# Decoding w_out's chunks into PSUM, transposing their finished high and low parts, and queueing the router's products further behind

## The chip, the cores and the metric

The kernel runs on one core of one Trainium2 chip. The metric is the device time of one execution in microseconds (us); a time of a kernel is the median of its runs. The engines are named as in the profile: PE (TensorE's matmuls), PEld (its weight loads), DVE (VectorE), ACT (ScalarE), POOL (GpSimd), SP (SyncE, which only issues transfers here).

## The reference, cut to what matters

Three layers follow one another: attention with a sliding window of 128 and 4 sink positions over 4 x 8 heads, 768 positions and 64 features; an MLP with a normalization; and a routed MLP with 8 experts, one per token.

```
x = attention(q, k, v)                      # (3072, 512)
h = x @ w_in                                # (3072, 1024)
solu = h * softmax(h)
ln = (solu - mean) / sqrt(var + 1e-6) * g_ln
x2 = ln @ w_out                             # (3072, 512)
logits = x2 @ w_gate                        # (3072, 8)
e = argmax(logits); gate = softmax(logits)[e]
out = gate * (relu(x2 @ w1[e]) @ w2[e])
```

`w_in` and `w_out` arrive as 64-bit floating-point numbers, seen as pairs of 32-bit integers, and the kernel has to turn them into 32-bit numbers itself.

## The kernel before, in words

Products that need nearly full 32-bit accuracy are made of three matmuls in the type fp32r on a high and a low part of each operand (high x high, high x low, low x high); the low part is the number less its rounded high part. Attention works on 32 units (128 query rows times three for two heads); a unit n has six score matmul groups `s` (lines 225, or 228 and 229 from unit 5 on), each followed on DVE by `copy_predicated` (L232) and a masked maximum (L233) and on ACT by an exponential (L235). The first MLP works on 24 tiles of 128 tokens (`m_in`: L453 to L455, `m_act`, `m_tr`: L502, `m_out`: L523 to L525), and the routed MLP comes last.

The weights of the first MLP are decoded while attention starts: `load_w_in` in eight chunks, then `load_w_out` in eight chunks of 128 x 512. `decode` loads a chunk (L333, issued from ACT's queue), scales its low words on ACT (L350) and joins them with the high words in two DVE instructions (L351 into the PSUM tile `dt`, L352 into the result). For `w_in` the result is a PSUM tile `dh`, for `w_out` an SBUF tile `dec`. ACT then rounds the high part (L362 for `wih`; L397, with `g_ln` as a factor by row, for `woh`), and DVE makes the low part (L363 `wil`, L398 `wol`).

Eight more columns of `woh` and `wol` carry `w_out @ w_gate`, so that the router's logits come out of the same matmuls as `x2`. They are made in two steps. `logits` transposes a decoded chunk (four fp32 transposes, L376) and copies it out on ACT (`xt`, L378). `logits2` multiplies it with `w_gate` (four fp32 matmuls of 8 columns, two records each in the trace, L384) and writes the eight columns (L387, L388 on DVE). In the loop over chunks, chunk k's step runs `logits2` of chunk k-2 and `logits` of chunk k-1; the last pieces come when the first `m_out` asks for them.

One table sets when the decoding's steps are written: `W_AT` lists after which exponential of attention each step comes (`weigh`), and its position fixes the L350 of a step behind that exponential. Within that program order a scheduler with a timeline of its own orders the instructions of each engine; on the chip each engine works through its list in that order. PSUM has 8 banks: 3 with the tag `psa` for attention's tiles (`s`, `skp`, `tp`, `av`), 5 with `psm` for the rest (`h`, `lt`, `x2`, `wt`, `wt2`, `dt`, `dh`). `skp` is the tile of the sink transposes (L270); ACT (L271) and DVE (L272, `skt`) read it before its bank is free.

Of the kernel before, what the change touches and what calls it, by code (L numbers as in the profile page):

```python
# [8 lines left out]
F32 = mybir.dt.float32  # L9
F32R = mybir.dt.float32r  # L10
BF16 = mybir.dt.bfloat16
I32 = mybir.dt.int32
U32 = mybir.dt.uint32
AF = mybir.ActivationFunctionType
ALU = mybir.AluOpType
# [15 lines left out]
WB, DB, EB, NXR, XGB = 4, 4, 2, 2, 6  # L31
PA = 3
NATP, LEAD = 5, 4
KLV = 2
LA = 2
TE = 18
# [1 line left out]
XT = 21  # L38
WSB = 6
HG, HD, HSTEP, FH = 1, 5, 2, 1  # L40
W_AT, RATIO = [1, 4, 7, 10, 13, 16, 19, 22, 24, 26, 27, 29, 30, 32, 33, 35], 0.7
ROOM = [608, 576, 512, 416, 384, 320, 288, 128]
CAPS = [-(-n // 128) * 128 for n in ROOM]
NBLK = sum(CAPS) // 128
# [4 lines left out]
SC_IN, SC_OUT, SX = 2.0 ** 8, 2.0 ** 64, 2.0 ** -8  # L49
# [3 lines left out]
def raw(ap):  # L53
    return ap.bitcast(F32)
# [3 lines left out]
def body(ctx, tc, a):  # L58
    nc = tc.nc
    V, A, G, T, SY = nc.vector, nc.scalar, nc.gpsimd, nc.tensor, nc.sync  # L60
# [3 lines left out]
    const = ctx.enter_context(tc.tile_pool(name="const", bufs=1))  # L64
# [18 lines left out]
    def ps(name):  # L83
        if name in ATT:
            a_ = True
        elif name in MOE:
            a_ = False
        else:
            flip[0] += 1
            a_ = flip[0] % 8 < PA  # L90
        return ps_p.tile([128, 512], F32, tag="psa" if a_ else "psm", name=name, bufs=PA if a_ else 8 - PA)
# [4 lines left out]
    ident = const.tile([128, 128], F32, name="ident")  # L96
# [45 lines left out]
    def in_win(out, r, tmp):  # L142
# [7 lines left out]
                           op1=ALU.mult)  # L150
# [30 lines left out]
    def a_split(n):  # L181
# [9 lines left out]
        A.activation(out=qA, in_=qd, func=AF.Copy)  # L191
        (V if n < KLV else G).tensor_tensor(out=kl, in0=kd, in1=raw(kA), op=ALU.subtract)
        G.tensor_tensor(out=lA, in0=qd, in1=raw(qA), op=ALU.subtract)  # L193
# [122 lines left out]

    g_sb = const.tile([128, 8], F32, name="g_sb")
    g_s = const.tile([128, 8], F32, name="g_s")
    g_l = const.tile([128, 8], F32, name="g_l")
    wg_sb = const.tile([128, 4, NE], F32, name="wg_sb")  # L320

    dec_p = [at]

    def dec_tile(name):
        return dec_p[0].tile([128, 512], I32, tag="dec", name=name, bufs=DB)

    ex, pin = [], [None]

    def decode(src, sb, flush):

        w = dec_p[0].tile([128, 512, 2], I32, tag="w64", name="w64", bufs=WB)
        with tc.issue_after(first_d.ins) if dec_p[0] is at else ExitStack():
            A.dma_start(out=w, in_=src)  # L333
        lo, hi = w[:, :, 0], w[:, :, 1]
        t0 = ps("dt").bitcast(I32)
        y = ps("dh") if sb is None else sb
        if flush:
            t = dec_tile("dec")
            V.tensor_scalar(out=t0, in0=hi, scalar1=0x07FFFFFF, scalar2=3, op0=ALU.bitwise_and,
                            op1=ALU.logical_shift_left)  # L340
            V.scalar_tensor_tensor(out=t, in0=hi, scalar=-0x40000000, in1=t0, op0=ALU.bitwise_and,
                                   op1=ALU.bitwise_or)
            A.activation(out=lo, in_=lo.bitcast(U32), func=AF.Copy, scale=2.0 ** -29)
            G.tensor_tensor(out=t, in0=t, in1=lo, op=ALU.add)
            x = ps("dh")
            A.activation(out=x, in_=hi.bitcast(F32), func=AF.Abs)
            V.scalar_tensor_tensor(out=y, in0=x, scalar=E_MIN, in1=t.bitcast(F32), op0=ALU.is_ge, op1=ALU.mult)
        else:
            with tc.issue_after(pin[0].ins) if pin[0] else ExitStack():
                A.activation(out=lo, in_=lo.bitcast(U32), func=AF.Copy, scale=LOW3)  # L350
            V.scalar_tensor_tensor(out=t0, in0=hi, scalar=3, in1=lo, op0=ALU.logical_shift_left, op1=ALU.bitwise_xor)  # L351
            V.scalar_tensor_tensor(out=y.bitcast(I32), in0=hi, scalar=-0x80000000, in1=t0, op0=ALU.bitwise_and,  # L352
                                   op1=ALU.bitwise_xor)
        return y
# [11 lines left out]

    def load_w_out(flush=False):
        sc = SC_OUT * (1.0 if flush else RAW)
        V.tensor_scalar(out=g_s, in0=g_sb, scalar1=sc, scalar2=None, op0=ALU.mult)
        V.tensor_scalar(out=g_l, in0=g_sb, scalar1=1.0 / SC_OUT, scalar2=None, op0=ALU.mult)  # L370

        def logits(k, x):

            t = ps("wt")
            for d in range(4):
                T.transpose(t[:, 128 * d:128 * d + 128], x[:, 128 * d:128 * d + 128], ident)  # L376
            xt = dec_tile("xt").bitcast(F32).rearrange("p (a b) -> p a b", a=4)
            A.activation(out=xt, in_=t.rearrange("p (a b) -> p a b", a=4), func=AF.Copy, scale=sc)  # L378
            return k, xt

        def logits2(k, xt):
            t = ps("wt2")
            for d in range(4):
                T.matmul(t[:, 0:NE], xt[:, d, :], wg_sb[:, d, :], start=(d == 0), stop=(d == 3))  # L384
            wp = t[:, 0:NE]
            gk = g_l[:, k:k + 1]
            V.tensor_scalar(out=woh[:, k, 0, 256:264], in0=wp, scalar1=gk, scalar2=None, op0=ALU.mult)  # L387
            V.scalar_tensor_tensor(out=wol[:, k, 0, 256:264], in0=wp, scalar=gk, in1=raw(woh)[:, k, 0, 256:264],  # L388
                                   op0=ALU.mult, op1=ALU.subtract)

        last = last2 = None
        for k in range(8):
            x = dec_tile("dec").bitcast(F32)
            decode(a["w_out"].bitcast(I32)[128 * k:128 * k + 128, :], x, flush)
            h_ = woh[:, k, :, 0:256]
            p2 = x.rearrange("p (a b) -> p a b", a=2)
            A.activation(out=h_, in_=p2, func=AF.Copy, scale=g_s[:, k:k + 1])  # L397
            V.scalar_tensor_tensor(out=wol[:, k, :, 0:256], in0=p2, scalar=g_s[:, k:k + 1], in1=raw(h_),  # L398
                                   op0=ALU.mult, op1=ALU.subtract)
            if last2:  # L400
                logits2(*last2)
                last2 = None
            if last:
                last2 = logits(*last)
            last = (k, x)
            yield 1.5
        logits2(*last2)
        logits2(*logits(*last))


    tri = const.tile([128, 128], BF16, name="tri")
# [871 lines left out]
    def weights():  # L1283
        yield from load_w_in()
        yield from load_w_out()
# [35 lines left out]
    wn = [0]  # L1321

    def weigh():
        while wn[0] < 16 and len(ex) > W_AT[wn[0]]:
            pin[0] = ex[W_AT[wn[0]]]
            step(gw, "w")
            wn[0] += 1
# [4 lines left out]
    while done_x[0] < 0:  # L1332
        step(ga, "a")
        cnt_ += 1
        if cnt_ == 12:
            late_loads()
        weigh()
# [4 lines left out]
    while True:  # L1342
        if a_open and ta <= tm * RATIO:
            d = step(ga, "a")
# [7 lines left out]
        d = step(gm, "m")  # L1352
# [7 lines left out]
        else:  # L1360
            d = step(ga, "a")
# [61 lines left out]
```

## Time and profile before

| | us |
|---|---|
| median of 3 runs (817.53 to 819.14) | 819.07 |
| the profiled execution's own time | 819.58 |
| its span in the trace | 817.4 |
| outside of the span | 2.2 |

How to read the profile: an engine's busy time is the time in which its instructions ran; a row's idle time is what the engine stood still just before it, with the instruction that released it. PEclk is the granted clock of TensorE as a share of 2.4 GHz; 0.50 is the lower level, 1.2 GHz. Matmuls are pipelined, so the cost of one in a row of equal ones is the distance from start to start, not the duration printed for it. "issue" as a releaser means that the profile shows nothing that the engine waited for.

### The profile page before, as it was taken

To read this page: it belongs to the slowest core of one execution; us is meant where nothing else is said; L and a number is where in the kernel's file an instruction comes from. 1 tells how busy PE (TensorE), PEld (TensorE's weight loads), DVE (VectorE), ACT (ScalarE), POOL (GpSimd) and SP (SyncE) were. 2 spreads that over 40 slices of the span, in tenths; PEclk is the share of its full clock that TensorE was granted. 3 is DMA by queue.
4 is the path that set the end of the run, shared out by engine and by line. 5 is a ranking of instruction groups with operands and counts; after the bars stand their busy time and mean duration, and the time that the engine had idled before them with its cause. 6 is when DMAs were issued, how large, how long until landed. Compare 5 with 4: busy or idle time off the path is not lost.

```text
span 817.4 us, 15512 instructions
## 1 busy us (share of the span) xinstructions
PE 776.4 (95%) x5003; PEld 670.3 (82%) x5003; DVE 478.5 (59%) x1766; ACT 461.9 (57%) x1236; POOL 355.4 (43%) x393
## 2 busy tenths in 40 slices
PE   4779999999999998999999998999999999999996
PEld 2457788897988887888988898888978888989885
DVE  6898666676758647766776566426333443435541
ACT  3677686675757848657766374235425243436442
POOL 3565354545354544555433121156235244535533
PEclk9968999999999999999999999999999999999998
DMA  8585355567557457474530271195375416663650
GB/s 272 186 260 155 92 150 119 131 135 142 126 132 156 117 113 161 121 154 102 142 85 27 32 239 44 46 330 204 101 254 193 156 63 213 225 211 96 227 172 28
DMA packets 78281, 120.82 MB, mean 148 GB/s; under 512 B 14122, under 2 KB 52524, under 8 KB 78192
## 3 DMA queue, kind: packets, MB, share of 16 engines
q1 hardware_dynamic: 70512, 97.48, 44.5%
q0 software_dynamic: 5088, 13.88, 4.8%
q10 hardware_dynamic: 2592, 8.39, 3.0%
q8 instruction: 42, 0.69, 0.4%
q14 instruction: 47, 0.39, 0.2%
HBM read 80.61 MB, written 13.28 MB: 115 GB/s over the span
## 4 chain that ended last, share of the span: by engine, by line
PE 78%; DVE 9%; DMA 5%; issue 3%; ACT 2%; POOL 1%; POOLq 0%; SPq 0%; ACTq 0%; DVEq 0%
PE ht L853 6%; PE ht L854 6%; PE ht L852 6%; PE x L523 5%; PE y L922 5%; PE h L453 5%; PE y L924 5%; PE y L923 5%; PE x L525 5%; PE x L524 5%; PE h L454 5%; PE av L306 4%; PE h L455 4%; PE s L228 3%; PE s L229 2%
## 5 line engine op out<-in xcount | busy, mean ns | idle before, releaser
L523 PE MATMUL x<-woh,lh 128*128 128x264 f32 (+1 forms) x384 | 111.5, 290 | 0.1
L525 PE MATMUL x<-woh,ll 128*128 128x264 f32 (+1 forms) x384 | 109.5, 286 | 0.0
L524 PE MATMUL x<-wol,lh 128*128 128x264 f32 (+1 forms) x384 | 109.0, 284 | 0.0
L235 ACT ACTIVATE P<-P,mx 128x144 f32<-128x144 f32 x192 | 78.5, 411 | 49.3 <-DVE mx L233 46.9
L760 ACT ACTIVATE wh<-wst 128x1024 fp32r<-128x1024 f32 x64 | 67.5, 1058 | 45.9 <-PE ht L853 26.6
L768 POOL TENSOR_TENSOR wl<-wst,wh 128x1024 fp32r<-128x1024 f32 x28 | 67.8, 2423 | 55.1 <-ACT wh L760 48.1
L853 PE MATMUL ht<-xel,wh 128*128 128x288 f32 (+5 forms) x256 | 81.2, 318 | 0.0
L854 PE MATMUL ht<-xeh,wl 128*128 128x288 f32 (+5 forms) x256 | 81.0, 318 | 0.0
L453 PE MATMUL h<-wih,bxh 128*128 128x512 f32 x192 | 79.0, 412 | 1.0 <-DVE ll L506 0.9
L768 DVE TENSOR_TENSOR wl<-wst,wh 128x1024 fp32r<-128x1024 f32 x36 | 53.1, 1478 | 45.9 <-ACT wh L760 44.0
L852 PE MATMUL ht<-xeh,wh 128*128 128x288 f32 (+5 forms) x256 | 79.7, 318 | 0.0
L922 PE MATMUL y<-wh,hh 128*128 128x512 f32 x192 | 77.2, 402 | 1.2 <-DVE hl L861 1.2
L454 PE MATMUL h<-wil,bxh 128*128 128x512 f32 x192 | 76.4, 398 | 0.0
L924 PE MATMUL y<-wh,hl 128*128 128x512 f32 x192 | 75.5, 395 | 0.0
L923 PE MATMUL y<-wl,hh 128*128 128x512 f32 x192 | 75.2, 392 | 0.0
L455 PE MATMUL h<-wih,bxl 128*128 128x512 f32 x192 | 74.3, 399 | 0.0
L523 PEld LDWEIGHTS x<-woh,lh 128*128 128x128 f32 x384 | 72.4, 188 | 1.7 <-DVE r L556 0.3
L232 DVE COPY_PREDICATED s<-pick,s 128x128 f32<-128x128 int32 x160 | 45.2, 292 | 48.6 <-PE s L229 45.9
L524 PEld LDWEIGHTS x<-wol,lh 128*128 128x128 f32 x384 | 72.4, 189 | 0.7
L525 PEld LDWEIGHTS x<-woh,ll 128*128 128x128 f32 x384 | 72.3, 189 | 0.6 <-issue 0.3
L193 POOL TENSOR_TENSOR lA<-qd,qA 128x384 fp32r<-128x384 f32 x27 | 28.1, 1042 | 95.3 <-ACT qA L191 75.0
L244 POOL TENSOR_TENSOR pk<-P,sm 128x768 f32<-128x768 f32 x32 | 47.6, 1487 | 45.2 <-DVE sm L242 38.8
(275 smaller groups left out, 2046.5 us busy)
## 6 DMA issues: line engine op xcount, KB each, us to landing
wst<-w SPq DMA_DIRECT2D x64, 512.0 KB
x_d<-xrow SPq DMA_DIRECT2D x24, 264.0 KB
qd<-qT SPq DMA_DIRECT2D x32, 192.0 KB
qB<-qA SPq DMA_DIRECT2D x54, 96.0 KB
lB<-lA SPq DMA_DIRECT2D x54, 96.0 KB
kd<-kx SPq DMA_DIRECT2D x16, 280.0 KB
w<-w_in ACTq DMA_DIRECT2D x8, 512.0 KB
w<-w_out ACTq DMA_DIRECT2D x8, 512.0 KB
```

The source lines that it names most:

```text
L453: T.matmul(h, xh[k], wih[:, k, cs], start=(k == 0), stop=False)
L454: T.matmul(h, xh[k], wil[:, k, cs], start=False, stop=False)
L523: T.matmul(p[:, 0:n], lh[:, k, :], woh[:, k, c, 0:n], start=(k == 0), stop=False)
L524: T.matmul(p[:, 0:n], lh[:, k, :], wol[:, k, c, 0:n], start=False, stop=False)
L525: mm = T.matmul(p[:, 0:n], ll[:, k, :], woh[:, k, c, 0:n], start=False, stop=(k == 7))
L768: return (G if c % 2 and r else V).tensor_tensor(out=l_, in0=st_w.pop((r, which, c)), in1=raw(h_), op=ALU.subtract)
L852: T.matmul(o, wh[:, k, fs], xh(k), start=(k == 0), stop=False)
L853: T.matmul(o, wh[:, k, fs], xl(k), start=False, stop=False)
L854: T.matmul(o, wl[:, k, fs], xh(k), start=False, stop=(k == 3))
L922: T.matmul(o, hh[:, k, sl], wh, start=(k == 0), stop=False)
L923: T.matmul(o, hh[:, k, sl], wl, start=False, stop=False)
L924: T.matmul(o, hl[:, k, sl], wh, start=False, stop=(k == 7))
```

## The change

Four things change. `decode` now puts `w_out`'s chunks into PSUM (`dh`), as it did `w_in`'s, and L397 and L398 read them there (L399 and L400 in the changed kernel). The four fp32 transposes of a decoded chunk become eight fp32r matmuls against an identity `ident_r`, two for each 128 columns, that add the finished high and low parts while transposing them (L378 in the changed kernel). `g_ln` is then already in the product, so the factor `g_l` goes. And the loop runs 8 + LAG steps with LAG = 3: `logits2` of chunk k-3, then `logits` of chunk k-1; three steps that have no chunk are written behind the exponentials 37, 38 and 40.

```
+LAG = 3
-W_AT, RATIO = [1, 4, ..., 33, 35], 0.7
+W_AT, RATIO = [1, 4, ..., 33, 35, 37, 38, 40], 0.7
...
     def load_w_out(flush=False):
         sc = SC_OUT * (1.0 if flush else RAW)
+        ident_r = dec_p[0].tile([128, 128], F32R, tag="idr", name="ident_r")
+        V.tensor_copy(ident_r, ident)
         V.tensor_scalar(out=g_s, in0=g_sb, scalar1=sc, scalar2=None, op0=ALU.mult)
-        V.tensor_scalar(out=g_l, in0=g_sb, scalar1=1.0 / SC_OUT, scalar2=None, op0=ALU.mult)
-        def logits(k, x):
+        def logits(k):
             t = ps("wt")
             for d in range(4):
-                T.transpose(t[:, 128 * d:128 * d + 128], x[:, 128 * d:128 * d + 128], ident)
+                for n, w in enumerate((woh, wol)):
+                    T.matmul(t[:, 128 * d:128 * d + 128], w[:, k, d // 2, 128 * (d % 2):128 * (d % 2) + 128], ident_r,
+                             start=(n == 0), stop=(n == 1))
...
-            A.activation(out=xt, in_=t.rearrange("p (a b) -> p a b", a=4), func=AF.Copy, scale=sc)
+            A.activation(out=xt, in_=t.rearrange("p (a b) -> p a b", a=4), func=AF.Copy)
...
-        last = last2 = None
-        for k in range(8):
-            x = dec_tile("dec").bitcast(F32)
-            decode(a["w_out"].bitcast(I32)[128 * k:128 * k + 128, :], x, flush)
...
-            if last2:
-                logits2(*last2)
-                last2 = None
-            if last:
-                last2 = logits(*last)
-            last = (k, x)
+        done = []
+        for k in range(8 + LAG):
+            if k < 8:
+                x = decode(a["w_out"].bitcast(I32)[128 * k:128 * k + 128, :], None, flush)
...
+            if k >= LAG:
+                logits2(*done.pop(0))
+            if 0 < k < 9:
+                done.append(logits(k - 1))
             yield 1.5
-        logits2(*last2)
-        logits2(*logits(*last))
```

Two places show what this does to the lists of the engines. The first is PE's list where attention passes from unit 4 (the last `s` with `kd,qd`) to unit 5 (the first with `kA,qA`). Before:

```order
L376 MATMUL wt_577<-ident_78,dec_549 128x128 x4
L270 MATMUL skp_616<-ident_78,psk_415 128x128 x3
L225 MATMUL s_622<-kd_445,qd_444 128x272
L225 MATMUL s_627<-kd_445,qd_444 128x272
L384 MATMUL wt2_598<-wg_sb_127,xt_582 128x8 x4
L376 MATMUL wt_605<-ident_78,dec_568 128x128 x4
L228 MATMUL s_729<-kA_679,qA_675 128x272
```

The same place now (the pairs of `woh` and `wol` into wt_577 come four times):

```order
L271 MATMUL skp_617<-ident_78,psk_414 128x128 x3
L226 MATMUL s_623<-kd_444,qd_443 128x272
L226 MATMUL s_628<-kd_444,qd_443 128x272
L378 MATMUL wt_577<-ident_r_546,woh_70 128x128
L378 MATMUL wt_577<-ident_r_546,wol_71 128x128
...
L378 MATMUL wt_602<-ident_r_546,woh_70 128x128
L229 MATMUL s_734<-kA_684,qA_680 128x272
L229 MATMUL s_771<-kB_685,qB_681 128x272
L230 MATMUL s_771<-kB_685,lB_683 128x272
L378 MATMUL wt_602<-ident_r_546,wol_71 128x128
```

The first chunk's transposes moved behind `skp` and the last two `s` of unit 4, its products with `w_gate` moved out of this place, and the second chunk's transposes are split around the first `s` of unit 5.

The second place is DVE's list at the same time, from the low part of `w_out`'s first chunk to `skt`, which frees the bank of `skp`. Before:

```order
L398 SCALAR_TENSOR_TENSOR wol_71<-dec_549,g_s_125,woh_70 128x2x256
L312 SCALAR_TENSOR_TENSOR bxl_530<-wt_520,bxh_529 128x384
L232 COPY_PREDICATED s_622<-pick_121,s_622 128x128
L352 SCALAR_TENSOR_TENSOR dec_589<-w64_590,dt_592 128x512
L232 COPY_PREDICATED s_627<-pick_121,s_627 128x128
L398 SCALAR_TENSOR_TENSOR wol_71<-dec_568,g_s_125,woh_70 128x2x256
L387 TENSOR_SCALAR woh_70<-wt2_598,g_l_126 128x8
L272 TENSOR_TENSOR skt_615<-skp_616,skt_615 128x384
```

The same place now:

```order
L400 SCALAR_TENSOR_TENSOR wol_71<-dh_552,g_s_125,woh_70 128x2x256
L233 COPY_PREDICATED s_623<-pick_121,s_623 128x128
L313 SCALAR_TENSOR_TENSOR bxl_529<-wt_519,bxh_528 128x384
L351 SCALAR_TENSOR_TENSOR dt_595<-w64_593 128x512
L233 COPY_PREDICATED s_628<-pick_121,s_628 128x128
L273 TENSOR_TENSOR skt_616<-skp_617,skt_616 128x384
```

The third chunk's second decoding step, the second chunk's low part and the first logits' copy moved behind `skt`, and the third chunk's first decoding step (ahead of the first row of the list before) now stands between the two.

## Rows read from the trace of the kernel before

**Rows 1.** The page: span, and PE's busy time, share and instructions.
```profile
span 817.4 us, 15512 instructions
PE 776.4 (95%) x5003; PEld 670.3 (82%) x5003; DVE 478.5 (59%) x1766; ACT 461.9 (57%) x1236; POOL 355.4 (43%) x393
```

**Rows 2.** Busy time by stretch: length, engines (instructions), granted clock, DMA share, GB/s.
```profile
46.00:83.00 37.00, 30.72 (x180) 25.86 (x177) 32.62 (x90) 26.12 (x69) 23.58 (x23) 0.77 0.72 202
83.00:460.00 377.00, 370.21 (x2611) 320.70 (x2610) 248.98 (x1111) 254.25 (x788) 175.54 (x210) 1.00 0.52 120
```

**Rows 3.** Whom PE waited for, 46 to 83 us: us in total, times, longest.
```profile
PE s L228 <- issue: 3.4, 1, 3.4
PE wt L384 <- ACT xt L378: 1.3, 2, 0.7
PE skp L270 <- POOL psk L253: 1.0, 1, 1.0
PE s L228 <- DVE mx L233: 0.5, 1, 0.5
```

**Rows 4.** PE's timeline: start, us, operation, shape, count, [idle before it, releaser].
```profile
50.35 0.63 PE L376 MATMUL wt<-ident,dec 128*128 128x128 f32 x4
54.40 0.57 PE L228 MATMUL s<-kA,qA 128*128 128x272 f32 x1 [3.41 <-issue]
...
66.25 0.63 PE L376 MATMUL wt<-ident,dec 128*128 128x128 f32 x4
66.64 0.47 PE L453 MATMUL h<-wih,bxh 128*128 128x512 f32 x1
...
73.82 1.06 PE L384 MATMUL wt<-wg_sb,xt 128*128 128x8 f32 x8 [0.51 <-ACT xt L378]
...
76.12 1.87 PE L384 MATMUL wt<-wg_sb,xt 128*128 128x8 f32 x8 [0.75 <-ACT xt L378]
...
110.10 0.28 PE L523 MATMUL x<-woh,lh 128*128 128x264 f32 x1
...
111.19 0.29 PE L523 MATMUL x<-woh,lh 128*128 128x264 f32 x1
```

**Rows 5.** DVE's timeline around the stall of PE.
```profile
49.88 1.21 DVE L398 SCALAR_TENSOR_TENSOR wol<-dec,g_s,woh 128x512 fp32r<-128x512 f32 x1
...
51.67 0.68 DVE L352 SCALAR_TENSOR_TENSOR dec<-w,dt 128x512 int32<-128x512 int32 x1
...
52.47 1.23 DVE L398 SCALAR_TENSOR_TENSOR wol<-dec,g_s,woh 128x512 fp32r<-128x512 f32 x1
53.62 0.21 DVE L387 TENSOR_SCALAR woh<-wt,g_l 128x8 fp32r<-128x8 f32 x1
53.76 0.54 DVE L272 TENSOR_TENSOR skt<-skp,skt 128x384 fp32r<-128x384 f32 x1
```

**Rows 6.** PE alone by stretches of 1 us, where the granted clock changes (columns: PE, clock, DMA).
```profile
52.00:53.00 1.00, 0.00 (x0) 0.50 1.02 377
62.00:63.00 1.00, 1.00 (x11) 0.90 1.00 316
76.00:77.00 1.00, 0.88 (x5) 0.50 0.09 29
82.00:83.00 1.00, 1.00 (x4) 0.66 0.76 173
```

**Rows 7.** The high and low parts of both weights: ns min/median/max, first and last start.
```profile
L398 DVE SCALAR_TENSOR_TENSOR wol<-dec,g_s,woh x8: 739/790/1595, 49.9 to 81.1; 128x512 fp32r<-128x512 f32 x8
L363 DVE SCALAR_TENSOR_TENSOR wil<-dh,wih x8: 676/684/691, 13.8 to 47.7; 128x512 fp32r<-128x512 f32 x8
L397 ACT ACTIVATE woh<-dec,g_s x8: 707/722/731, 47.3 to 80.4; 128x512 fp32r<-128x512 f32 x8
L362 ACT ACTIVATE wih<-dh x8: 572/592/597, 13.2 to 45.5; 128x512 fp32r<-128x512 f32 x8
```

**Rows 8.** DVE groups of 46 to 83 us: count, busy us, mean ns, idle before.
```profile
L398 DVE SCALAR_TENSOR_TENSOR wol<-dec,g_s,woh 128x512 fp32r<-128x512 f32 x8 | 7.9, 982 | 0.9 <-ACT woh L397 0.9
```

## What was predicted, ahead of the run

> **What bounds the kernel now.** I began with the busy times. PE is busy for 776.4 of 817.4 us [rows 1], so the end is PE's list: its work plus the time in which it stands or runs at the lower clock. The view by stretches tells where that second part lies. From 83 to 460 us, where attention and the first MLP run side by side, PE is busy for 370.21 of 377 us at a granted clock of 1.00; from 46 to 83 us, where w_out is decoded, it is busy for 30.72 of 37 us at 0.77 [rows 2]. So whatever the change does early moves the end almost one for one, because PE has no slack behind it, and there are two things to look at in the 37 us: 6.3 us of idle time and the clock.
>
> The idle time has four owners [rows 3]. The largest is one gap of 3.4 us. The profile gives it no releaser, but PE's timeline and DVE's tell one. PE finishes the transposes of 50.35 at 50.98 and starts the first score of unit 5 at 54.40 [rows 4]; `skt` on DVE ends at 53.76 + 0.54 = 54.30 [rows 5]. `skp` and the last two scores of unit 4 hold the three banks of attention, so the next score needs the bank that `skt` frees, and `skt` stands on DVE behind two low parts of w_out and a decoding step. The second owner is 1.3 us in which the router's products wait for `xt`, twice, at 73.82 (0.51) and 76.12 (0.75) [rows 4]: transposes, ACT's copy, products, transposes, copy, products, one after the other with little else in the list.
>
> The clock falls to the lower level twice. After PE had been less than fully busy and then idle, it reads 0.50 from 52 us on and comes back in the stretch of 62 us (0.90); after the two waits for `xt` it reads 0.50 from 76 us and comes back within the stretch of 82 us (0.66) [rows 6]. A reading of 0.90 between 0.50 and 1.00 means a return at 62.2, one of 0.66 a return at 82.7.
>
> **The change part by part.** All sums are of the profiled execution (819.58 us, of which 817.4 are the span), which lies 0.5 us above the median.
>
> *New work on PE.* 32 transposes go, 64 fp32r products of 128 columns come. Four transposes take 66.64 - 66.25 = 0.39 us from start to start, 0.098 us each, at full clock [rows 4]. The trace has no fp32r product of 128 columns. The nearest row with the same weight load is the `x` product with 264 columns: nine in 111.19 - 110.10 = 1.09 us, 0.121 us each [rows 4]. This is the upper end; the lower end is the transpose's 0.098, which loads and streams a block of the same shape. I take 0.11, in the middle, since the columns are as few as the transpose's and the weight type is that of `x`. 64 x 0.11 - 32 x 0.098 = 7.0 - 3.1 = **+3.9 us** (3.1 to 4.6). The products with `w_gate` stay as many.
>
> *The gap of 3.4 us.* In the new list three things no longer stand ahead of `skt` [rows 5]: the third chunk's second decoding step, 0.68 us of which some 0.6 are not covered by the next instruction's start; the second chunk's low part from 52.47 to 53.62, 1.15; the logits' copy from 53.62 to 53.76, 0.14. The first low part, 1.21 us long here, shrinks by 0.5 (next paragraph). `skt` begins at about 53.76 - 1.9 - 0.5 = 51.4 and PE resumes at 52.0 instead of 54.4: **-2.4 us**. What is late next: the new transposes of the second chunk stand right behind that score, and need the second low part, which now follows `skt` on DVE and ends at about 52.9. Ends: 0, if the next DVE result is as late as `skt` was, and -3.4.
>
> *Low parts and high parts out of PSUM.* With the chunk in SBUF a low part took 0.739 to 1.595 us, 7.9 us for eight, mean 0.982 [rows 7, 8]; the same instruction on w_in's chunks, which lie in PSUM, took 0.676 to 0.691 in all eight cases [rows 7]. DVE gains 8 x (0.982 - 0.684) = 2.4 us, ACT 8 x (0.722 - 0.592) = 1.0 us [rows 7]. DVE is busy for 32.62 of these 37 us [rows 2], so the first is worth something, but only through PE's waits, and it is not counted again beside them. The copy that makes `ident_r` (a third of `skt`'s width, so under 0.54 us [rows 5]) comes once, ahead of the first transposes, where DVE's idle 4.4 us of the stretch can hide it; without that cover it would cost its own length.
>
> The Trainium skill's page "Perfetto Trace Analysis", section "Optimizing Scalar/DVE Operations", speaks against this part: it gives VectorE a larger fixed cost per instruction on PSUM (about 125 ns) than on SBUF (about 60 ns). By it the eight low parts would take 0.5 us more in all, an estimate from that page; rows 7 say the opposite for this very instruction, whose slowest run from PSUM is faster than the fastest from SBUF, and the measurement decides.
>
> *The queue for the router.* With the products three chunks behind, `xt` is made long before they come up: the waits of 0.51 and 0.75 go, **-1.3 us**. A new one can take their place: the transposes needed only the decoded chunk, and now need its high part (0.59 us on ACT) and its low part (0.68 us on DVE) as well [rows 7], 1.3 us later. Behind a waiting transpose on PE stand scores and `h` products, and DVE waits for those scores. Ends: 0, and 2.6 us for two such waits in full; I take one of half that size, **+0.7 us**, since the transposes still come one step behind their chunk.
>
> *The clock.* In the first slow stretch PE restarts 2.4 us sooner; if the return comes as much sooner, 2.4 us of work at half rate become 1.2: **-1.2 us**. Ends: 0, and -3.9 if the clock did not fall at all, half of the 62.2 - 54.4 = 7.8 us that PE then worked. The second stretch, 82.7 - 76 = 6.7 us, cost 3.35 us. It follows the waits for `xt`, which go, but other gaps may stand there; I take half, **-1.7 us**, ends 0 and -3.4.
>
> *The steps that moved.* The three added steps hold products and their copies only, no transfers; w_out's loads stay in ACT's queue in the old order. All the router's work is now ahead of the first `x` product, before which some of it was queued; the number of instructions ahead of the end is the same either way, so this is 0.
>
> Sum: 3.9 - 2.4 - 1.3 + 0.7 - 1.2 - 1.7 = **-2.0 us**. DVE allows it: 2.4 us less of work and 4.4 us of idle time in a stretch that has to shrink by 3.5 us, since about 1.5 us of the new PE work come behind it.
>
> **The rivals.** *The clock holds.* If the filled gaps keep PE at the upper level all along, both slow stretches vanish: -2.0 - (3.9 - 1.2) - (3.4 - 1.7) = -6.4, 812.7 us. For it: both falls came after gaps that the change fills. Against it: the first came a mere 1.0 us after PE ran dry at 50.98 [rows 4], and at that point the new list is hardly fuller than the old. The Trainium skill's page "TensorE: Matmul & The Clock Gate", section "Part 4: PE-mode transpose", has a rule that would lead here: transposes do not bring the engine to full clock, and the new ones are ordinary products. No row here shows the one without the other.
>
> *The gap moves.* DVE, busy at 88% here [rows 2], still hands out the banks late; the transposes' wait takes the place of the waits for `xt`, and the second slow stretch stays: 3.9 - 2.4 - 1.3 + 0.7 - 1.2 = -0.3, 818.8 us.
>
> *Slower: a bank too few.* The chunk now holds a `psm` bank from its second decoding step to the end of its low part. Five banks serve `dt`, `dh`, `wt`, `wt2` and the two `h` tiles that start at 66.64 [rows 4]. If a late low part keeps an `h` or a decoding step without a bank, PE waits for one high and low part, 1.3 us [rows 7], at each of the last three chunks, and these gaps keep the second slow stretch: -2.0 + 3.9 + 1.7 = +3.6, 822.7 us. It decides once idle time and lost clock from 46 us to the end of the decoding shrink by less than the 3.9 us of new work. Against it: w_in's chunks lived in the same banks without a long wait of PE, but then no `h` did.
>
> **How the numbers follow.** The forecast is 819.07 - 2.0 = 817.1 us, chance 0.45; clock holds 0.13; gap moves 0.20; slower 0.22. The range leaves out half of the first rival and somewhat under half of the last: 812.6 to 822.0. A measurement of this kernel tells about 0.2%, 1.6 us, from no change, that is 817.4 to 820.7. Of the forecast's chance two thirds lie below it and a third within: faster 0.30 + 0.13 = 0.43, same 0.15 + 0.20 = 0.35, slower 0.22.
>
> **What would show it.** In the profile after: the gap before the first score of unit 5 under 1.5 us; no wait of the products for `xt`; low parts all near 0.68 us; a granted clock clearly above 0.77 in the decoding's stretch; 64 products at 0.10 to 0.12 us from start to start. It is wrong if the products take more than 0.12 us each at full clock, if PE waits for `wol` or a `psm` bank for over 2 us in all, or if idle time behind 83 us, 6.8 us here [rows 2], changes by more than 1.5 us, since the scheduler orders that part anew as well and none of my terms speaks of it.

## The result, and the profile after

The changed kernel took **826.87 us** (median of four runs, 825.62 to 832.11) against 819.11 us for the kernel before beside it (817.53 to 820.13): ratio **1.0109**, 95% interval 1.0062 to 1.0155. The forecast was 817.1 us with a range of 812.6 to 822.0. It was wrong, and on the wrong side. The profiled execution took 826.23 us, 824.5 of them the span, 7.1 more than before.

The page of the kernel after, span and PE (its columns are those of [rows 1]):

```profile
span 824.5 us, 15583 instructions
PE 781.2 (95%) x5035; PEld 674.4 (82%) x5035; DVE 473.7 (57%) x1766; ACT 460.3 (56%) x1236; POOL 352.6 (43%) x393
```

Busy time by stretch, kernel after (length, PE, PEld, DVE, ACT, POOL with instructions, granted clock, DMA share, GB/s):

```profile
46.00:83.00 37.00, 30.46 (x198) 26.52 (x195) 29.28 (x87) 25.93 (x67) 21.13 (x23) 0.82 0.72 198
83.00:460.00 377.00, 368.89 (x2610) 320.55 (x2609) 246.30 (x1114) 253.33 (x791) 175.79 (x210) 1.00 0.54 120
460.00:825.00 365.00, 352.04 (x2135) 309.47 (x2133) 163.11 (x431) 154.45 (x298) 136.58 (x94) 0.99 0.48 158
```

Against [rows 2] the decoding's stretch looks a little better: 198 PE instructions in place of 180, clock 0.82 for 0.77, DVE 3.3 us less busy. So far the forecast seems to hold. In detail it does so for the two gaps it was about. PE's timeline of the kernel after (start, us, operation, shape, count, [idle before it, releaser]):

```profile
49.98 0.27 PE L378 MATMUL wt<-ident_r,woh 128*128 128x128 f32 x1
...
50.53 0.28 PE L378 MATMUL wt<-ident_r,wol 128*128 128x128 f32 x1
...
52.49 0.56 PE L229 MATMUL s<-kA,qA 128*128 128x272 f32 x1 [1.50 <-DVE skt L273]
...
53.60 0.41 PE L378 MATMUL wt<-ident_r,woh 128*128 128x128 f32 x1
53.81 0.41 PE L378 MATMUL wt<-ident_r,wol 128*128 128x128 f32 x1
```

The gap ahead of unit 5's first score shrank from 3.41 us [rows 4] to 1.50, and the releaser that was inferred, `skt`, is named. The new products come 0.11 us apart (50.53 - 49.98 for five), but 0.21 where the clock is low (53.60 to 53.81). Whom PE waited for from 46 to 83 us shows what came in exchange:

```profile
PE skp L271 <- POOL psk L254: 2.1, 1, 2.1
PE s L229 <- DVE skt L273: 1.5, 1, 1.5
PE s L229 <- DMA qA<-qA: 1.3, 1, 1.3
PE s L230 <- DMA lA<-lA: 1.2, 1, 1.2
PE s L229 <- DVE sm L243: 0.5, 1, 0.5
```

Against [rows 3] the waits for `xt` are gone and the long gap is halved, but the wait for `psk` grew from 1.0 to 2.1, and two transfers of q and its low part, which nobody waited for before, take 2.5 us. None of this explains 7 us. Two other places account for most of it, and neither is in w_out.

**The routed MLP is slower, matmul by matmul.** PE's groups by form, 530 to 800 us (line, operation, out<-in, shape, count | busy us, mean ns of one | idle before), first of the kernel before:

```profile
L922 PE MATMUL y<-wh,hh 128*128 128x512 f32 x177 | 71.1, 402 | 0.0
L923 PE MATMUL y<-wl,hh 128*128 128x512 f32 x178 | 69.7, 392 | 0.0
L853 PE MATMUL ht<-xel,wh 128*128 128x416 f32 x32 | 11.2, 351 | 0.0
```

and of the kernel after:

```profile
L920 PE MATMUL y<-wh,hh 128*128 128x512 f32 x178 | 72.3, 406 | 1.2 <-DVE hl L859 1.2
L921 PE MATMUL y<-wl,hh 128*128 128x512 f32 x178 | 70.3, 395 | 0.0
L851 PE MATMUL ht<-xel,wh 128*128 128x416 f32 x32 | 11.3, 354 | 0.0
```

Three or four nanoseconds each, on instructions that the change does not touch, at a granted clock of 1.00 in both.

**The handover to the routed MLP.** ScalarE's timeline of the kernel before, then of the kernel after, where it splits the first expert's weights (`wh`):

```profile
478.57 1.06 ACT L760 ACTIVATE wh<-wst 128x1024 fp32r<-128x1024 f32 x1 [2.80 <-DMA wst<-w]
```

```profile
482.06 1.06 ACT L758 ACTIVATE wh<-wst 128x1024 fp32r<-128x1024 f32 x1 [3.69 <-DMA wst<-w]
...
484.88 1.06 ACT L758 ACTIVATE wh<-wst 128x1024 fp32r<-128x1024 f32 x1 [1.40 <-DMA wst<-w]
485.84 0.19 ACT L480 ACTIVATE sc<-sc 128x1 f32<-128x1 f32 x1
485.94 1.06 ACT L503 ACTIVATE lh<-lt 128x512 fp32r<-128x512 f32 x2
```

ScalarE now waits twice for weights, 5.1 us in place of 2.8, with `lh` of a late tile behind the second wait. PE waits for that tile, and then its clock falls (PE's timeline, and PE in slices of 1 us: length, busy, clock, DMA share, GB/s):

```profile
486.57 0.39 PE L521 MATMUL x<-woh,lh 128*128 128x264 f32 x1 [1.16 <-ACT lh L503]
487.96 0.39 PE L523 MATMUL x<-woh,ll 128*128 128x264 f32 x1 [0.88 <-DVE ll L504]
```

```profile
487.00:488.00 1.00, 0.12 (x2) 1.00 0.38 143
488.00:489.00 1.00, 1.00 (x7) 0.76 0.60 118
489.00:490.00 1.00, 1.00 (x6) 0.50 0.61 205
490.00:491.00 1.00, 1.00 (x7) 0.50 0.79 222
```

In the profile of the kernel before the clock stays at 1.00 throughout this stretch.

### The profile page after: what moved, and what is told of

The parts are those of the page before. It is cut to its first block, busy times and chain, and to the rows that moved or that the text cites. A ratio compares the mean times of both kernels' runs of the same rounds, so it can differ in the third digit from the quotient of the medians.

```text
span 824.5 us, 15583 instructions
## 1 busy us (share of the span) xinstructions
PE 781.2 (95%) x5035; PEld 674.4 (82%) x5035; DVE 473.7 (57%) x1766; ACT 460.3 (56%) x1236; POOL 352.6 (43%) x393
## 4 chain that ended last, share of the span: by engine, by line
PE 78%; DVE 7%; DMA 7%; issue 3%; ACT 2%; POOL 1%; SPq 1%; POOLq 0%; ACTq 0%; DVEq 0%
PE ht L851 6%; PE ht L852 6%; PE ht L850 6%; PE x L521 5%; PE x L523 5%; PE y L920 5%; PE y L922 5%; PE y L921 5%; PE x L522 5%; PE h L451 5%; PE h L452 4%; PE h L453 4%; PE av L307 4%; PE s L229 2%; PE s L230 2%
## 5 line engine op out<-in xcount | busy, mean ns | idle before, releaser
L521 PE MATMUL x<-woh,lh 128*128 128x256 f32 (+1 forms) x384 | 111.8, 291 | 1.3 <-ACT lh L503 1.2
L523 PE MATMUL x<-woh,ll 128*128 128x256 f32 (+1 forms) x384 | 110.2, 288 | 0.9 <-DVE ll L504 0.9
L522 PE MATMUL x<-wol,lh 128*128 128x256 f32 (+1 forms) x384 | 109.4, 285 | 0.0
L766 DVE TENSOR_TENSOR wl<-wst,wh 128x1024 fp32r<-128x1024 f32 x36 | 54.9, 1530 | 46.0 <-ACT wh L758 46.0
```

The lines of the kernel that those rows point to most:

```text
L521: T.matmul(p[:, 0:n], lh[:, k, :], woh[:, k, c, 0:n], start=(k == 0), stop=False)
L522: T.matmul(p[:, 0:n], lh[:, k, :], wol[:, k, c, 0:n], start=False, stop=False)
L523: mm = T.matmul(p[:, 0:n], ll[:, k, :], woh[:, k, c, 0:n], start=False, stop=(k == 7))
L766: return (G if c % 2 and r else V).tensor_tensor(out=l_, in0=st_w.pop((r, which, c)), in1=raw(h_), op=ALU.subtract)
```

## The experiments

Kernels were run in groups, each on one chip beside the kernel before, whose median went from 817.5 to 823.7 us from group to group; so ratios to it are what is compared. A ratio is worked out from the runs of the group and need not be the quotient of the two medians. "Lost to the clock" is the sum, over slices of 1 us, of PE's busy time times (1 - granted clock).

### The change taken apart

**Parts alone, in the old loop and 16 steps** (the chunk in PSUM and the new transposes stay):

```
-        done = []
-        for k in range(8 + LAG):
+        last = last2 = None
+        for k in range(8):
...
+            if last2:
+                logits2(*last2)
+                last2 = None
+            if last is not None:
+                last2 = logits(last)
+            last = k
+            yield 1.5
+        logits2(*last2)
+        logits2(*logits(last))
```

> The kernel before, with the PSUM decode and the transposes of the finished parts, but with the old loop: products one chunk behind, the last two chunks' products in the sixteenth step, 16 steps. Its order of work behind the w_out stage is nearly that of before (the changed kernel's is not). Theory 'order': the changed kernel's extra 7 us are 3.9 us of new TensorE work, less 2.2 us that the first 83 us give back in clock and idle time, and about 5 us from the other order behind 83 us that the three extra steps set off; then this kernel has only the first two, and stands at 820 to 822 us, 4 to 6 below the changed kernel. Rival 'work': the loss comes with the new transposes themselves and what they push; then this kernel stands within 1.5 us of the changed one, 825 to 828.

Measured: 829.25 us, ratio 1.0111 (1.0085 to 1.0138).

**The queue alone** (chunk in SBUF, fp32 transposes, old scale; loop of the changed kernel with LAG = 3 and its 19 steps):

```
-            x = dec_tile("dec").bitcast(F32)
...
+                x = kept[k] = dec_tile("dec").bitcast(F32)
...
-            if last2:
-                logits2(*last2)
+            if k >= LAG:
+                logits2(*done.pop(0))
+            if 0 < k < 9:
+                done.append(logits(k - 1, kept.pop(k - 1)))
```

> The kernel before, SBUF decode and fp32 transposes kept, with nothing but the new queue: products two chunks behind and 19 steps. No new TensorE work. Theory 'order': the idle time of the changed kernel behind 83 us comes with this alone; 822 to 825 us, and a span with 2 to 5 us more idle time or slow clock between 110 and 520 us than before. Rival 'work': the queue alone costs nothing, and takes the wait for xt away: 817 to 819.5 us.

Measured: 823.08 us, ratio 1.0039 (1.0024 to 1.0054).

**The old transposes twice:**

```
-                T.transpose(t[:, 128 * d:128 * d + 128], x[:, 128 * d:128 * d + 128], ident)
+                for _ in range(2):
+                    T.transpose(t[:, 128 * d:128 * d + 128], x[:, 128 * d:128 * d + 128], ident)
```

> The kernel before with each of the 32 transposes of w_out's chunks issued twice: 32 more of about 0.1 us at full clock or 0.2 at half, 3.1 to 6 us of TensorE work in the same place as the changed kernel's new work, and nearly no other change of order. Where TensorE sets that stage, 822 to 825 us (both theories want this: work counts one to one). If the added work only fills gaps there, or brings the clock up, 818 to 820.5 us, and then the 3.9 us of new work are no part of the loss.

Measured: 820.86 us, ratio 1.0008 (0.9989 to 1.0027).

**The high part only** (the changed kernel; it leaves the low parts out of the router's logits):

```
-                for n, w in enumerate((woh, wol)):
-                    T.matmul(t[:, 128 * d:128 * d + 128], w[:, k, d // 2, 128 * (d % 2):128 * (d % 2) + 128], ident_r,
-                             start=(n == 0), stop=(n == 1))
+                T.matmul(t[:, 128 * d:128 * d + 128], woh[:, k, d // 2, 128 * (d % 2):128 * (d % 2) + 128], ident_r,
+                         start=True, stop=True)
```

> The changed kernel with only the product of the high part in each transpose; it leaves the low parts out of the router's logits. 32 products fewer, about 3.5 us of TensorE work less, and no wait for the low parts; the 19 steps stay. Theory 'order': 822 to 824 us, still above the kernel before by 3 to 5 us. Rival 'work': the loss goes with the work and its pushes, 819 to 821 us. Rival 'bank wait' (the low parts hold the PSUM banks): below 819 us.

Measured: 826.06 us, ratio 1.0084 (1.0054 to 1.0115).

The theory of the order missed the first of these: with the old steps, and nearly the old order, the time was not 820 to 822 us but stood at the changed kernel's ratio. It met the second: `lag_only` has no new work, and none of its tiles of the routed MLP moved (see below), yet the queue with its 19 steps, and the order that comes of them, cost it 823.08 - 819.41 = 3.7 us. So the order is one part of the loss and not the whole. My accounting of the work fell with the last two: 32 more transposes cost next to nothing, and 32 products fewer brought nothing that can be told from the scatter. The rows of 46 to 83 us of `twice`, of the parts alone and of the queue alone bear on why PE work there has no simple price:

```profile
46.00:83.00 37.00, 31.47 (x211) 27.34 (x212) 33.31 (x92) 26.31 (x69) 24.33 (x25) 0.91 0.75 211
```

```profile
46.00:83.00 37.00, 32.00 (x181) 27.32 (x181) 28.14 (x84) 24.79 (x63) 20.78 (x23) 0.72 0.72 194
```

```profile
46.00:83.00 37.00, 31.95 (x213) 26.88 (x210) 33.49 (x101) 27.74 (x73) 21.54 (x23) 0.91 0.69 197
```

PE is busy for about the same time in the first two, but at 0.91 the one gets 31 instructions more done than [rows 2] of the kernel before, and at 0.72 the other only one more. In the profile of `twice` the clock paid for the doubled transposes; in that of `parts16` it did not pay for the new products. One reservation: the profile of `twice` is of the fastest of its twelve executions (817.31 us, with a granted clock of 0.993 over the whole span; the others have 0.983 to 0.989), so 0.91 is more than its usual share. `lag_only`, with no transpose added, has 0.91 as well.

Of these four kernels, the two with the chunk in PSUM also had the slow `y`, the two with the chunk in SBUF did not. That led to the next four.

### The place of tiles in SBUF

The change deletes `g_l`, 32 bytes a partition. In the built programs every tile of the pools behind it then begins 32 bytes earlier: `hh` moves from byte 24,992 to 24,960, that is from 32 to 0 within its 64 bytes, and so do `hl`, `xeh`, `xel`, `wih`, `bxh`. The expert weights (`wh`, `wl`) lie in a pool at the other end, at 163,808, and stay at 32. A tile that nobody uses moves them without altering a single instruction or its place in any queue.

**The change with `g_l` back:**

```
     g_s = const.tile([128, 8], F32, name="g_s")
+    g_l = const.tile([128, 8], F32, name="g_l")
```

> The changed kernel with one unused tile of 32 bytes a partition (g_l, which the change had taken out) back in its place: the same instructions in the same order on all five engines, only the tiles that lie behind it in SBUF begin 32 bytes further on, where they began before the change. Theory 'place': the slower matmuls of the routed MLP (products y of 512 columns 406/395/397 ns in the changed kernel, 402/392/395 before; ht of 416 columns 354 for 351) come from that shift; they go back to 402/392/395 and 351, the part of the span behind the last logits product is 1.5 to 3.5 us shorter, and the time 822.5 to 825. Rival: the rate comes from something else that the change sets off; then nothing moves, 825.5 to 827.

Measured: 825.39 us, ratio 1.0034 (1.0000 to 1.0068), on a chip where the kernel before took 823.71.

**The kernel before with one such tile more:**

```
     g_s = const.tile([128, 8], F32, name="g_s")
+    g_p = const.tile([128, 8], F32, name="g_p")
```

> The kernel before with one more unused tile of 32 bytes a partition in the same place: the same instructions in the same order, the tiles behind it begin 32 bytes further on, and stand in their 64 bytes where the changed kernel has them. Theory 'place': y takes 406/395/397 ns, ht of 416 columns 354, and the time rises by 1.5 to 3.8 us, to 820.5 to 823.5, without any other change. Rival: no effect, 818.5 to 820.

Measured: 825.23 us, ratio 1.0055 (1.0018 to 1.0092).

**The weights moved as well, and the weights alone** (an unused tile at the end of their pool; `w0h0` has `g_p` besides):

```
         look_at_weights()
         assert seen[0] == 16 and not look
+        pool2["w"].tile([128, 8], F32, name="w_p")
```

> before_pad with a second unused tile of 32 bytes, at the end of the pool of the expert weights (wh, wl): the weights now begin at 0 in their 64 bytes, as hh, hl, xeh and xel do; instructions and order are those of the kernel before. In the kernel before all stand at 32, in the changed kernel the weights at 32 and the rest at 0. Theory 'pair' (a matmul is slower where its two operands stand differently): y back at 402/395/392 ns or below, time 818 to 820.5. Theory 'zero' (operands that begin at 0 are slower): y at 406 or above, 822 to 826.

Measured: 823.97 us, ratio 1.0013 (0.9977 to 1.0050).

> The kernel before with only that second tile: the expert weights at 0, hh, hl, xeh and xel at 32. Theory 'pair': slower as in the changed kernel, y 406/397/395 ns, 821 to 824. Theory 'zero': y, whose moving operand is the weights, slower, ht as before (351 ns at 416 columns).

Measured: 825.10 us, ratio 1.0024 (0.9990 to 1.0058).

In these two groups the kernel before itself scattered by more than 10 us, and the times alone settle little. The groups of matmuls do. In this order: the change with `g_l` back (both at 32), the kernel before with a tile more (weights 32, `hh` 0), the weights alone moved (0 and 32), both moved (0 and 0):

```profile
L922 PE MATMUL y<-wl,hh 128*128 128x512 f32 x180 | 70.5, 392 | 0.0
L852 PE MATMUL ht<-xel,wh 128*128 128x416 f32 x32 | 11.2, 351 | 0.0
```

```profile
L924 PE MATMUL y<-wl,hh 128*128 128x512 f32 x177 | 69.9, 395 | 0.0
L854 PE MATMUL ht<-xel,wh 128*128 128x416 f32 x32 | 11.3, 354 | 0.0
```

```profile
L923 PE MATMUL y<-wl,hh 128*128 128x512 f32 x175 | 69.1, 395 | 0.0
L853 PE MATMUL ht<-xel,wh 128*128 128x416 f32 x32 | 11.3, 354 | 0.0
```

```profile
L924 PE MATMUL y<-wl,hh 128*128 128x512 f32 x181 | 70.5, 390 | 0.0
L854 PE MATMUL ht<-xel,wh 128*128 128x416 f32 x32 | 11.2, 352 | 0.0
```

Where the two operands stand alike, `y` of `wl` and `hh` takes 390 to 392 ns; where they differ, 395, whichever of them moved. Theory "pair" holds and "zero" falls. The `h` products of the first MLP bear it out from the other side: both of their operands moved together, and the rows of 110 to 455 us read 409, 396 and 398 ns before, 407, 396 and 398 after. What it costs in the `y` stretch is read from the first `y` product to the end of the span: in the seven profiles with unlike operands 293.3 to 295.1 us, in the thirteen with like ones 289.8 to 292.3; means 294.5 and 291.5, so **3.0 us**.

### The steps

**Sixteen steps** (`after_gl`, with the last products all in the sixteenth; `W_AT` has its old 16 entries):

```
-            yield 1.5
+            if k < 7 or k == 7 + LAG:
+                yield 1.5
```

> after_gl with 16 steps in place of 19: the products of the last chunks all fall into the sixteenth step, as they did before the change; the queue is the changed kernel's up to there. The order behind 83 us is another than in either kernel. Theory 'order' (the three extra steps cost 2 to 3 us at the handover to the routed MLP): 2 to 3 us below after_gl, 820 to 822. Rival: the handover costs the same in any order of this kind, within 1 us of after_gl.

Measured: 825.28 us, ratio 1.0027 (0.9995 to 1.0058), the same as `after_gl` on that chip (1.0034). Ahead of the handover sixteen steps do not bring the old order back; from the 900th `x` product on PE's list is the old one but for a few places, and the handover showed the fall of the clock here too (1.5 us lost).

**The products one chunk behind, as before** (LAG = 2, 18 steps):

> The changed kernel with the products one chunk behind, as before the change, and 18 steps; the order differs from the changed kernel's by a few places in the w_out stage alone. If the deeper queue is worth what the old loop with the same transposes lost against the changed kernel (829.25 for 826.23), 828 to 830; if that was the steps' doing, 825.5 to 827.5.

Measured: 829.99 us, ratio 1.0109 (1.0059 to 1.0159): the changed kernel's ratio. The deeper queue by itself brings nothing that can be told from this.

### The handover

`TE` is the tile behind which the head of the routed MLP is planned and its first weights are asked for. With one earlier the first of these loads is issued 9 us sooner in the traces (at 457.77 us in `before_te2`, at 466.99 in the kernel before):

```
-TE = 18
+TE = 17
```

> after_gl with the routed MLP's head planned after tile 17 in place of tile 18, some 15 us earlier, so that the first expert's weights are loaded long before ScalarE splits them. Theory 'handover' (the split that waits for weights holds ScalarE's work for the last tiles, and TensorE falls to half clock at 488 us): the dip at 488 goes, and the time is 2 to 3 us below after_gl, against before_te's difference to the kernel before. Rival: the dip comes from the order of the last tiles itself; it stays, within 1 us.

Measured: 821.29 us, ratio 0.9966 (0.9932 to 1.0000).

> The kernel before with the same earlier head: the control for after_gl_te. It has no dip at the handover to lose: within 1.5 us of before, either way.

Measured: 820.57 us, ratio 0.9990 (0.9954 to 1.0026).

Then the changed kernel and its two repairs on one chip (the kernel before there: 817.50 us):

> The changed kernel itself, on the chip of the next three runs: 5 to 9 us above the kernel before (1.007 to 1.011 of it).

Measured: 827.64 us, ratio 1.0126 (1.0103 to 1.0148).

> after_gl again, beside the changed kernel: same instructions in the same order, tiles 32 bytes further on. Theory 'place': 2.5 to 4 us below the changed kernel, 1.003 to 1.006 of the kernel before. If the two are within 1 us, the difference between the earlier runs was that between two chips.

Measured: 823.27 us, ratio 1.0067 (1.0041 to 1.0094): **4.4 us** for the place.

> after_gl_te again, beside after_gl. Theory 'handover': 2 to 4 us below after_gl, and within 1.5 us of the kernel before (0.997 to 1.001 of it): then place and handover are the whole loss, and what the change does ahead of 110 us comes to nothing. Rival: the new TensorE work ahead of 110 us costs something that stays, 1.002 to 1.005 of the kernel before.

Measured: 815.27 us, ratio 0.9973 (0.9960 to 0.9986): another **8.0 us**, twice what I expected.

> The changed kernel with the head planned after tile 17, and with the place mended the other way: the expert weights moved to 0 in their 64 bytes by an unused tile at the end of their pool, so that both operands begin at 0. Theory 'pair': as fast as after_gl_te or up to 1.5 us faster (y took 401/390/393 ns with both at 0, 402/392/395 with both at 32), and below the kernel before by 0 to 4 us.

Measured: 814.62 us, ratio 0.9967 (0.9953 to 0.9981). The place can be mended from either side, and this version of the change beats the kernel before, which still has the late head.

And the control, beside the repaired change (the kernel before there: 820.03 us):

> The control again, beside after_gl_te. In the trace of before_te the stretch from the x product number 1008 to the last is 3.3 us shorter than before, as in after_gl_te2 (3.7). If that is its worth, 0.996 to 0.998 of the kernel before, and the earlier head helps both kernels; what it saves the changed kernel beyond that (after_gl_again to after_gl_te2: 8.0 us) is the wait and the fall of the clock that the change brought. Rival: the kernel before gains nothing, 0.999 to 1.001, and the whole 8.0 us are the change's.

Measured: 816.20 us, ratio 0.9952 (0.9937 to 0.9966).

> after_gl_te again, on the chip of before_te2: with place and handover alike in both, what is left between the two is the w_out stage. If the new TensorE work stays a cost there, 1.5 to 3.5 us above before_te2; if the stage gives as much back in idle time as it takes, within 1 us of it; if the forecast's net gain is real, 1 to 2.5 us below.

Measured: 818.16 us, ratio 0.9974 (0.9959 to 0.9989).

So the earlier head is worth 3.8 us to the kernel before as well; by this the other 4.2 us of the 8.0 had come with the change, a difference between two chips. And with place and handover alike, the changed kernel is **2.0 us slower** than the old one. That is the w_out stage and the other order behind it together; no run separates the two. By its ratio the best kernel of all is the one before with the earlier head, though its interval overlaps that of `after_w0_te`. Busy time from 455 to 520 us, of the kernel before, the changed one, the changed one repaired, the kernel before with the earlier head:

```profile
455.00:520.00 65.00, 62.19 (x432) 58.17 (x431) 41.49 (x194) 32.59 (x82) 10.02 (x11) 1.00 0.37 99
```

```profile
455.00:520.00 65.00, 61.10 (x418) 56.21 (x415) 37.45 (x168) 32.86 (x83) 8.79 (x10) 0.97 0.36 95
```

```profile
455.00:520.00 65.00, 64.75 (x459) 60.36 (x456) 41.95 (x194) 33.35 (x84) 9.40 (x11) 1.00 0.29 99
```

```profile
455.00:520.00 65.00, 63.76 (x442) 60.20 (x441) 41.71 (x197) 31.59 (x81) 9.47 (x10) 1.00 0.31 99
```

PE stands for 2.8, 3.9, 0.25 and 1.2 us of the 65, and only the changed kernel runs below 1.00. The last 144 starts of `x` products (three tiles) span 30.3, 32.1, 26.5 and 27.0 us. Over all profiles with the late head they span 32.7 us in the mean of the eight with another order than the old one, 31.4 in the six with the old one (`parts16` and `twice` among them). So of the 8.0 and the 3.8 us the stretch shows 6.2 and 4.4, and of the 4.2 between them only 1.8; where the rest lies is open.

The fall of the clock is not the change's alone. Among the late heads it stands in six of the seven profiles with the changed kernel's order of the last tiles, and in three of the seven with the old order there (`w0h0`, `w0h32`, `after_gl_16`). It stands in none of six with the early head. And it does not come in every execution of a program: `after_again` has none here.

## Why the prediction was wrong, point by point

The loss on one chip, 827.64 - 817.50 = 10.1 us, is made of 4.4 (place), 4.2 (the part of the handover that came with the change) and 2.0 (what is left, the w_out stage and the order behind it): 10.6. The 2.0, and the 3.8 within the 4.2, come from another chip. Each has an uncertainty of some 2 us, and the loss in the first comparison was 7.8, so the shares are rough. The traces show a piece of each: 3.0 us for the place, 1.8 for the handover, and for the third the start of the last 144 `x` products, which lies 3.0 us later in the mean of the eight profiles of the changed kernel and its repairs (487.2) than in that of six of the kernel before and its variants (484.2). `parts16` is not closed by these shares: the place and the third are 6.4 of its 9.8 us. It loses 10.6 us to the clock from 46 to 110 us, where those six lose 7.4 in the mean.

**The step that failed first is "the steps that moved", put at 0.** It counted the instructions ahead of the end and not their order. The order from 110 us on was another, and the handover had a wait of 2.8 us on ScalarE with a queue behind it that I never looked at. The runs showed 4.2 us there, of which the traces of the handover show 1.8, and 3.7 us for the queue and its order alone in `lag_only`. The prediction had named the part behind 83 us as what would make it wrong, since none of its terms spoke of it. But its sign was the idle time of 83 to 460 us, which rose from 6.8 to 377.00 - 368.89 = 8.1, by less than the 1.5 it asked for; the handover lies behind that stretch. A term should have looked there: the row of `wh` waiting for its transfer stood in the trace of before.

**A term was missing: the place.** The prediction has no term for the deletion of `g_l`. It moved one operand of the routed MLP's matmuls and not the other, and the runs showed 4.4 us (3.0 of them in the `y` stretch).

**The clock, put at -1.2 - 1.7 = -2.9, came to nothing.** The profile after shows 5.5 us lost to the clock from 46 to 110 us against 7.2 before, which looks like half of it; but over the eight profiles of the changed kernel and its repairs the mean is 7.6 (5.5 to 9.0), over six of the kernel before and its variants 7.4 (6.7 to 8.3). The second slow stretch did go, as these slices of the kernel after show beside [rows 6]:

```profile
64.00:65.00 1.00, 1.00 (x7) 0.50 1.02 368
65.00:66.00 1.00, 0.48 (x3) 0.86 0.94 298
76.00:77.00 1.00, 1.00 (x9) 1.00 0.88 308
82.00:83.00 1.00, 1.00 (x10) 1.00 0.46 98
```

but the first lasted until 65 us in place of 62, and in other profiles until later; the waits for `psk` and for transfers stand ahead of it and inside it.

**The idle time, -2.4 - 1.3 + 0.7 = -3.0, was right in size:** from 46 to 110 us PE stands for 5.1 us in the mean of those eight profiles and 7.8 in the six, -2.7. The mechanisms were right for the two gaps removed, and wrong for the wait that came: not for low parts but for `psk`, `qA` and `lA`. It comes back later: from 110 to 455 us the eight profiles stand for 7.9 us, the six for 6.1, and in six of the eight the clock also falls there for one or two short stretches, in none of the six. That loses 1.5 us in the mean. So the 2.7 - 0.2 = 2.5 us won up to 110 us are lost again, 1.8 + 1.5 = 3.3, before the handover; what the prediction took to be won for good was not.

**The new work, +3.9, had the right price per product** (0.11 us at full clock). With the idle time and the clock about even, it is the likely owner of the 2.0 us. But neither doubling the transposes nor dropping half of the products moved the time by what its count says, so that is argued and not shown.

**The low parts were right in direction:** from PSUM they take 741 to 753 ns,

```profile
L400 DVE SCALAR_TENSOR_TENSOR wol<-dh,g_s,woh x8: 741/750/753, 49.0 to 81.1; 128x512 fp32r<-128x512 f32 x8
```

8 x (0.982 - 0.750) = 1.9 us less of DVE's work against [rows 8], where 2.4 were forecast. The forecast took 0.684 from `wil` as the same instruction, but `wil` is made with a constant factor and without `g_s`; with `g_s` it is 0.750. The Trainium skill's page "Perfetto Trace Analysis", section "Optimizing Scalar/DVE Operations", gives VectorE the larger fixed cost on PSUM; by it they would have become longer. The mean went the other way, from 982 to 750 ns; the shortest hardly moved, from 739 to 741.

**The rivals.** "The gap moves" is nearest to what the w_out stage did, with `psk` and two transfers as the new owners, though it was priced at no change and 2.0 us were lost. "Slower: a bank too few" came nearest in time (822.7), but the waits of 46 to 83 us above name none for a `psm` bank; the change was slower for other reasons, so that nearness is luck. "The clock holds" did not happen. The rule behind it, of the Trainium skill's page "TensorE: Matmul & The Clock Gate", section "Part 4: PE-mode transpose", would have ordinary products bring the engine to full clock where transposes do not. No run here bears it out: with twice the transposes the granted clock of 46 to 83 us is 0.91, with products in their place 0.72 to 0.82. Nor does this refute it, since `lag_only` has 0.91 with the transposes of the kernel before.

## What to carry to other kernels

A change that deletes a small constant moves every tile behind it: compare the mean duration of matmuls that the change does not touch, and if they differ at the same clock, put the bytes back before judging the change. A change that adds steps to a planner's list has an effect wherever another queue waits for a load with work behind it, so the waits with the least slack far behind the edit belong into the sum. And idle time that is filled is not clock that is won: the two have to be counted apart, over more than one profile.

## What the runs showed of the hardware that was not expected

The place of a matmul's two operands shows in its time. A `y` matmul of 512 fp32r columns takes, in the three forms `wh,hh`, `wl,hh` and `wh,hl`, 401 to 404, 390 to 392 and 393 to 395 ns where its two operands begin alike within 64 bytes of their partitions, and 405 to 407, 395 and 397 where they differ by 32. An `ht` matmul of 416 columns takes 351 or 352 and 354, one of 288 columns 293 to 296 either way. Only starts at 0 and 32 within the 64 bytes were tried. The Trainium skill's page "SBUF — State Buffer", section "Operand start alignment", asks only that an operand begin at a multiple of its element size; every kernel here keeps to that, so the rule does not tell the fast from the slow. Why the pair matters, no run here shows. `w0h0` is a partial exception: its `ht` of 512 columns took 395 ns, like the kernels with unlike operands, while `after_w0_te`, with both operands at 0 as well, reads 388 to 394.

Left untried: `lag_only`, the deeper queue with the chunk in SBUF, with the earlier head. It lost only 3.0 us to the clock from 46 to 110 us, against 7.4, and gave it back behind 110 us, where the clock fell twice; with the earlier head it might keep some of it.
